# Attention and two expert networks on one core: the second network's weights prepared in alternating units, with five split tiles and merged stores

## The chip, the core and the metric

The kernel runs on one core of a Trainium2 chip. The core has a matrix engine (TensorE, PE in the profile, with its weight loads as PEld), three engines for elementwise work (VectorE or DVE, ScalarE or ACT, GpSimd or POOL), and SyncE (SP), which here only issues DMAs. ACT issues DMAs too, between its own instructions. The metric is the time on the device in microseconds (us), median of several runs.

## The reference

Attention with 8 batches, 8 heads, 576 positions and 64 channels is followed by two networks on 4608 tokens of width 512. All inputs are float32.

```python
def _attn_ref(q, k, v):
    q_s = softmax(q, axis=-1)            # over the 64 channels
    k_s = softmax(k, axis=2)             # over the 576 positions
    kv = np.einsum('bhsd,bhse->bhde', k_s, v)
    return np.einsum('bhsd,bhde->bhse', q_s, kv)

def _moe_ref(x, w_in, w_out):            # 512 -> 2048 -> 512
    r = np.maximum(x @ w_in, 0.0)
    return (r * r) @ w_out

def _moe2_ref(x, w_gate, w_val, w_out, rms_g):   # 512 -> 1536 -> 512
    xn = x / np.sqrt(np.mean(x * x, axis=-1, keepdims=True) + 1e-06) * rms_g
    g, val = xn @ w_gate, xn @ w_val
    return (g / (1 + np.exp(-g)) * val) @ w_out
```

(The two softmax calls stand for the written-out maximum, exponential and division of the reference.)

## The kernel before

Every product is done in float32r with both operands split into a high and a low half (`a = hi + lo`), in three passes: hi x hi, hi x lo, lo x hi (`PASSES`). A split is a copy by ACT, which rounds to the high half, and a subtraction by DVE, which gives the low half.

The tokens are cut into 9 blocks of 512. For blocks 0 to 6 the first network runs in units `(j, c)`, 16 to a block, numbered `i = 16 * j + c`: `p1_A` is the product with a column of `w_in` (12 matmuls into `ps_h`), `p1_hi` and `p1_lo` take relu (`r`), square (`r`) and the split (`w`) on ACT and DVE one unit later, and `p1_B` multiplies by `w_out` into `acc` two units later. The attention of a later block runs in small steps between these (`attention(2 * i)` and `attention(2 * i + 1)` in each unit): `ke` and `qt` are exponentials on ACT, `mcb`, `qm`, `qs`, `qn`, `kt` come from DVE, and PE does `ps_kb`, `ps_q`, `ps_kv` and `ps_x`. The last two blocks and the whole second network use a scheme with 7 products for 8, with sums of halves of the weights in place of the weights.

Weights come in as 64-bit numbers in their words and have to be made into float32 and split first. `d_load` fetches a raw tile of 512 KB (SP), `d_words` makes two words' tiles of it (ACT), `d_float` a float32 tile (DVE, three passes). `tick` does one such step for several tiles, each at its own stage. For the first network this is done in blocks 0 and 1, and the split tiles are kept in DRAM as `wd_i` and `wd_o`. For the second network 36 steps follow in blocks 1 to 5; `n_ticks(i)` says by which unit how many have been done. After four of them `d_quad` has four quarters `a11` to `a22` of a weight and puts eleven entries into the queue `outs`: four sums on DVE (`s1` to `s4`) and seven splits (`d_out`). `d_light` does the like for the first network's weights, whose sums are needed for the last two blocks: it takes a tile that `p1_A` or `p1_B` has just used, adds its halves on DVE, and puts four subtractions and two splits into `sums_l`.

A split by `d_out` writes a tile `so` of 512 KB, one of four that are taken in turn: ACT copies, DVE subtracts at the unit's end (`lows`), and `send` puts it in the list `late`, from which `flush` issues the store on ACT's queue in the next unit: to `wl_i` or `wl_o` (the first network's sums), to `wd_v` (the second network's output weights), or to `wd_t` (its input weights: 42 tiles, the halves of each go to two places in two DMAs of 256 KB). SP loads all of them back later through a ring of 7 tiles `ws`.

Within an engine the instructions run in the order in which the code emits them. A unit emits, in this order: `p1_A`, `p1_hi` of the unit before, `attention(2 * i)`, `p1_B`, `p1_lo`, the steps of the preparation, `flush`, up to three entries of `sums_l` and up to two of `outs` (three in block 6), `attention(2 * i + 1)`, and `lows`. Each DMA, of SP or ACT, counts its landing on one of eight counters, in turn, and waits at its issue until the one before it on that counter has landed.

Of the kernel before, what the change touches and what calls it, by code (L numbers as in the profile page):

```python
# [8 lines left out]
F32 = mybir.dt.float32  # L9
F32R = mybir.dt.float32r  # L10
# [4 lines left out]
ALU = mybir.AluOpType  # L15
# [25 lines left out]
def attention_moe_kernel(  # L41
# [14 lines left out]
    ve, se, ge, te = (  # L56
        InOrder(tc, engine, pinned) for engine in (nc.vector, nc.scalar, nc.gpsimd, nc.tensor)
    )
    B, H, S, D = q.shape
    NT, DM = out.shape  # L60
    P = 128
# [5 lines left out]
    FF1 = w_in.shape[0]  # L67
    NQ = 2 * w_gv.shape[2] // 3
# [5 lines left out]
    const = ctx.enter_context(tc.tile_pool(name="const", bufs=1))  # L74
# [7 lines left out]

    ident = const.tile([P, P], F32, name="ident")
    ones_r = const.tile([P, P], F32R, name="ones_r")
    neg_r = const.tile([P, P], F32R, name="neg_r")
    eps_sb = const.tile([P, 1], F32, name="eps_sb")
    g_sb = const.tile([P, KD], F32, name="g_sb")
    mask = const.tile([P, 2, D], F32, name="mask")
# [12 lines left out]
    turns = {"a": 0, "so": 0, "d": 0, "t": 0}  # L101
# [40 lines left out]
    PROD = ("a11", "s2", "s1", "a12", "s3", "s4", "a22")  # L142
# [16 lines left out]
    def spread(keys, n):  # L159
# [5 lines left out]
    wd = {  # L165
        key: tc.dram_tile([P, 1024], F32, name="wd_" + "_".join(map(str, key)))
        for key in order1 + order2
    }
    SUMS = {"i": ("s2", "s4", "s3", "s1"), "o": ("s2", "s3", "s4", "s1")}
    wsum = {n: tc.dram_tile([P, 4, FF1 // 2, 512], F32, name=f"wl_{n}") for n in SUMS}  # L170
    pools = {}
# [23 lines left out]
    def flat(t):  # L195
        return t.rearrange("p b f -> p (b f)").bitcast(F32)
# [98 lines left out]
    def d_float(key):  # L295
        s, n = words.pop(key)
        if key[0] in ("i", "o"):
            turns["t"] += 1
            t = pools["d"].tile([P, 512], U32, tag=f"t{turns['t'] % 2}", name="t", bufs=1)
        else:  # L300
            n2 = 2 if key[0] in ("12", "21") else 1
            t = pools["q"].tile([P, 512], U32, tag=f"t{key[0]}", name=f"t{key[0]}", bufs=n2)
        sb = s.bitcast(U32)
        ve.tensor_scalar(
            out=t,
            in0=sb,
            scalar1=3,
            scalar2=0x7FFFFFFF,
            op0=ALU.logical_shift_left,
            op1=ALU.bitwise_and,  # L310
        )
        ve.scalar_tensor_tensor(
            out=t, in0=sb, scalar=0x80000000, in1=t, op0=ALU.bitwise_and, op1=ALU.bitwise_or
        )
        ti = t.bitcast(I32)
        ve.tensor_tensor(out=ti, in0=ti, in1=n, op=ALU.add)
        floats[key] = t.bitcast(F32)
# [6 lines left out]
    def flush(all=False):  # L324
        for x in late:
            x[0] -= 1
        while late and (late[0][0] < 0 or all):
            _, key, t = late.pop(0)
            if key[0] in ("i", "o"):
                tc.keep_in_program_order(se.dma_start(out=wd[key], in_=flat(t)))  # L330
                continue
            if key[0] == "L":
                _, kind, x, n = key
                tc.keep_in_program_order(
                    se.dma_start(
                        out=wsum[kind][:, 2 * x : 2 * x + 2, n],
                        in_=flat(t).rearrange("p (g f) -> p g f", g=2),
                    )
                )
                continue  # L340
            if key[1] >= NQ:
                to = [wd["v", BPROD.index(key[0]) * NQ // 2 + key[1] - NQ]]
            else:
                to = []
                for g in range(2):
                    p, at = divmod(g * NS + PROD.index(key[0]), 2)
                    to.append(wd["t", key[1], p][:, at * 512 : (at + 1) * 512])
            for g, o in enumerate(to):
                src = flat(t) if len(to) == 1 else flat(t)[:, g * 512 : (g + 1) * 512]
                tc.keep_in_program_order(se.dma_start(out=o, in_=src))  # L350

    def d_hi(key):
        t = slot_tile(key) if key in res1 else ring_tile()
# [15 lines left out]
    def d_light(kind, j, c):  # L369
        n, r = divmod(c, 2)  # L370
        if (kind, j) not in (("i", 2 + n % 2), ("o", 4 + n % 2)):
            return
        t = pools["d"].tile([P, 512], U32, tag=f"t{r}", name="t", bufs=1).bitcast(F32)
        w = wt[kind, c].bitcast(F32)
        ve.tensor_tensor(out=t, in0=w[:, 0], in1=w[:, 1], op=ALU.add)
        halves_l[r] = t
        if r == 0:
            return
        f = [halves_l.pop(0), halves_l.pop(1)]
        half = [f[0][:, 0:HF], f[0][:, HF:], f[1][:, 0:HF], f[1][:, HF:]]  # L380
        a11, a12, a21, a22 = half if kind == "i" else (half[0], half[2], half[1], half[3])

        def sub(out, in0, in1, op=ALU.subtract):
            sums_l.append(lambda: ve.tensor_tensor(out=out, in0=in0, in1=in1, op=op))

        sub(a22, a21, a22, ALU.add)
        sub(a21, a11, a21)
        sub(a11, a22, a11)
        sub(a12, a12, a11)
        for x in (1, 0):  # L390
            d_out(("L", kind, x, n), lambda x=x: f[x], sums_l)

    def d_out(key, f, outs=outs):
        def run():
            turns["so"] += 1
            t = pools["q"].tile([P, 2, 512], F32R, tag=f"so{turns['so'] % 4}", name="so", bufs=1)
            src = f().rearrange("p (g f) -> p g f", g=2)
            ts = t.rearrange("p g (a f) -> p g a f", a=2)
            se.activation(out=ts[:, :, 0], in_=src, func=AF.Copy)

            def low():
                ve.tensor_tensor(
                    out=ts[:, :, 1], in0=src, in1=ts[:, :, 0].bitcast(F32), op=ALU.subtract
                )
                send(key, t, 0)

            lows.append(low)

        outs.append(run)

    def d_quad(key):
        n, c = key
        if n != "11":
            return
        f = {"a" + b: floats.pop((b, c)) for b in ("11", "12", "21", "22")}

        def d_sum(name, in0, in1, op):
            def run():
                f[name] = pools["q"].tile([P, 512], F32, tag=name, name=name, bufs=1)
                ve.tensor_tensor(out=f[name], in0=f[in0], in1=f[in1], op=op)  # L420

            outs.append(run)

        def out(name):
            d_out((name, c), lambda: f[name])

        d_sum("s1", "a21", "a22", ALU.add)
        out("a22")
        d_sum("s3", "a11", "a21", ALU.subtract)
        d_sum("s2", "s1", "a11", ALU.subtract)  # L430
        out("a11")
        out("s1")
        out("s3")
        d_sum("s4", "a12", "s2", ALU.subtract)
        out("s2")
        out("a12")
        out("s4")
# [332 lines left out]
        return pool.tile([P, 512], F32, tag=tag, name=name)  # L770

    qfs, kT, eks = ({} for _ in range(3))
    qps = []

    def s_loadvl(j):
        nc.sync.dma_start(
# [58 lines left out]
    def s_xn(j, hp):  # L835
        t, ps = xts[j, hp]
        if j == 0:
            f = s_tile([P, T], "xf", 2)
            se.activation(out=f, in_=ps, func=AF.Copy)
            xts[j, hp] = t, f  # L840
        else:
            te.matmul(ps, neg_r, t[:, 0], start=False, stop=True, skip_group_check=True)

    def s_xl(j, hp):
        t, f = xts[j, hp]
# [101 lines left out]
    def p1_hi(j, c):  # L947
        if not ahead(j, ("i", c)):
            p1_r(j, c)
        r = kept.pop((j, c))  # L950
        ghl[1, j, c] = r
        split_hi(ghl, (1, j, c), g_tile(c % 4))
# [418 lines left out]
    def n_ticks(i):  # L1371
        if i < FF1:
            return min(NJ1 + 3, 4 + sum(d <= i for d in due.values()))
        at = [2 * FF1 - 1]
        at += [n for n in range(2 * FF1, 5 * FF1) if n % 4 > 1 or n in (48, 49, 64, 65)]
        at += [n for n in range(5 * FF1, JU * FF1) if n % 4 > 1 or n in (80, 81)]
        at = at[: 4 * NC2 + 1]
        return NJ1 + 4 + sum(n <= i for n in at)

# [59 lines left out]
    with ExitStack() as ctx_a:  # L1439
# [23 lines left out]
        for j in range(2):  # L1463
            t = s_tile([P, 2 * NP, D], f"vl{j}", 1)
            ge.memset(t[SR:P], 0.0)
            vl.append(t)
        make_identity(nc, ident)
        ge.tensor_scalar(
            out=neg_r, in0=ident, scalar1=-1.0, scalar2=0.0, op0=ALU.mult, op1=ALU.add
        )  # L1470
# [110 lines left out]
        for i, (j, c) in enumerate(units[: JU * FF1]):  # L1581
# [24 lines left out]
            p1_A(j, c)  # L1606
            for x in last:
                p1_hi(*x)
            if c == LAG:
                p1_out(j - 1)  # L1610
            attention(2 * i)
# [8 lines left out]
            if j == 1 and 4 <= c < 4 + NTAG:  # L1620
                key = res1[c - 4]
                tc.keep_in_program_order(nc.sync.dma_start(out=wd[key], in_=flat(wt[key])))
            while ticks[0] < n_ticks(i):
                tick()
            if ticks[0] > NJ1 + 4:
                flush()
            for queue, n in ((sums_l, 3), (outs, 2 if j < JU - 1 else 3)):
                for _ in range(min(n, len(queue))):
                    queue.pop(0)()
            attention(2 * i + 1)  # L1630
# [159 lines left out]
```

## Time and profile before

| | us |
|---|---|
| median of 3 runs | 1702.78 (1701.0 to 1706.39) |
| profiled execution | 1712.44 |
| its span, first to last instruction | 1710.7 |
| PE busy in the span | 1656.7 (97%) |
| VectorE busy | 1222.2 (71%) |
| ScalarE busy | 876.8 (51%) |
| moved by DMA | 434.09 MB, mean 254 GB/s |

Shares of busy time are means over the whole program, which has parts of different kinds: the start with the first attention heads, the units of blocks 0 to 6 up to about 757 us, and the second scheme from there to the end. A stretch has to be read for itself. The line of a helper (L34) stands for nearly every instruction, so that groups are told apart by what they write and read, `out<-in`. "Idle before, released by" says what ended the last wait; ACTq and SPq are the queues' own instructions, DMA issues among them. PEclk is the granted clock of TensorE.

### The profile page before, as it was taken

Reading aid. Unit: us, or ns where it says so; the run is one execution under the profiler, and the core shown is the slowest. Engines: PE = TensorE matmul, PEld = TensorE weight load, DVE = VectorE, ACT = ScalarE, POOL = GpSimd, SP = SyncE. Lnnn points to the kernel's source line nnn. Section 1 sums busy time; section 2 is a strip of 40 time slices with the busy share of each in tenths; the row PEclk is TensorE's granted clock in tenths of the full one; section 3 lists DMA queues with packets and bytes.
Section 4 is the critical chain, followed back from the end, with each engine's and each line's share of the span. In section 5 each row is a group of like instructions: output and inputs, shape, how many; then the busy total and the mean of one; then the engine's idle time right before and its main releaser. Section 6 shows DMA issues by size and latency. Waiting matters only on the chain.

```text
span 1710.7 us, 23162 instructions
## 1 busy us (share of the span) xinstructions
PE 1656.7 (97%) x8190; PEld 1367.9 (80%) x8190; DVE 1222.2 (71%) x1936; ACT 876.8 (51%) x1414; POOL 25.0 (1%) x41
## 2 busy tenths in 40 slices
PE   7999999988889999999999999999999999999999
PEld 4888887776667787888788888888888888888898
DVE  7986467877877887445786678667866786668666
ACT  7875445646555565348745444444444444423433
POOL 5000000000000000000000000000000000000000
PEclk9999999999999999999999999999999999999999
DMA  8987989999999998546668556865686558555798
GB/s 259 314 288 251 296 258 306 331 357 313 304 322 315 329 351 272 202 149 214 187 198 278 192 185 202 271 203 186 190 267 216 188 188 256 202 190 195 230 393 302
DMA packets 224898, 434.09 MB, mean 254 GB/s; under 512 B 86416, under 2 KB 117136, under 8 KB 223632
## 3 DMA queue, kind: packets, MB, share of 16 engines
q1 hardware_dynamic: 197088, 369.82, 66.5%
q10 hardware_dynamic: 27696, 62.79, 9.7%
q8 instruction: 66, 1.08, 0.2%
q14 instruction: 48, 0.39, 0.1%
HBM read 347.08 MB, written 85.46 MB: 253 GB/s over the span
## 4 chain that ended last, share of the span: by engine, by line
PE 77%; DMA 11%; DVE 6%; ACT 4%; issue 1%; SPq 0%; ACTq 0%; POOL 0%; POOLq 0%; DVEq 0%
PE ps_x L34 21%; PE ps_y L34 18%; PE ps_h L34 11%; PE acc L34 10%; PE ps_v L34 10%; PE ps_w L34 5%; DMA wd_t<-so 3%; DMA qt<-in_q 2%; DVE t L34 1%; DMA wl_o<-so 1%; DVE so L34 1%; ACT r L34 1%; DMA ws<-wd_i 1%; DMA raw<-in_w_gv 1%; DMA wd_v<-so 1%
## 5 line engine op out<-in xcount | busy, mean ns | idle before, releaser
L34 PE MATMUL ps_h<-x,ws 128*128 128x512 f32 x1008 | 249.5, 398 | 8.6 <-ACT r L34 8.6
L34 PE MATMUL acc<-w,ws 128*128 128x512 f32 x1008 | 248.3, 396 | 0.0
L34 PEld LDWEIGHTS ps_h<-x,ws 128*128 128x128 f32 x1008 | 190.1, 191 | 50.1 <-ACT r L34 10.2
L34 PEld LDWEIGHTS acc<-w,ws 128*128 128x128 f32 x1008 | 189.3, 190 | 39.7
L34 PE MATMUL ps_y<-xo,ws 128*128 128x512 f32 (+1 forms) x816 | 194.3, 373 | 0.3 <-ACT sa L34 0.3
L34 PE MATMUL ps_v<-xo,ws 128*128 128x512 f32 (+1 forms) x816 | 194.1, 373 | 0.2
L34 PE MATMUL ps_x<-ob,ws 128*128 128x512 f32 x768 | 177.4, 389 | 0.0
L34 PE MATMUL ps_x<-xo,ws 128*128 128x512 f32 (+1 forms) x720 | 169.0, 370 | 0.0
L34 PEld LDWEIGHTS ps_y<-xo,ws 128*128 128x128 f32 x816 | 145.0, 188 | 29.1 <-ACT sa L34 0.8
L34 PEld LDWEIGHTS ps_v<-xo,ws 128*128 128x128 f32 x816 | 144.9, 188 | 29.2 <-issue 0.3
L34 PEld LDWEIGHTS ps_x<-ob,ws 128*128 128x128 f32 x768 | 144.2, 188 | 30.0
L34 DVE TENSOR_TENSOR u<-ps_y,p 128x512 f32<-128x512 f32 (+1 forms) x136 | 87.5, 643 | 104.9 <-PE ps_y L34 77.8
L34 ACT ACTIVATE ob<-gs 128x1024 fp32r<-128x1024 f32 (+1 forms) x105 | 102.2, 974 | 113.1 <-PE ps_x L34 52.1
L34 PEld LDWEIGHTS ps_x<-xo,ws 128*128 128x128 f32 x720 | 127.1, 188 | 24.5
L34 DVE TENSOR_TENSOR ob<-gs,ob 128x1024 fp32r<-128x1024 f32 (+1 forms) x105 | 116.7, 1112 | 30.0 <-ACT ob L34 29.5
L34 PE MATMUL ps_y<-ob,ws 128*128 128x512 f32 x576 | 133.8, 390 | 0.7 <-DVE ob L34 0.7
L34 ACT ACTIVATE p<-ps_x 128x512 f32<-128x512 f32 (+1 forms) x74 | 41.7, 564 | 174.6 <-PE ps_x L34 172.3
L34 PEld LDWEIGHTS ps_y<-ob,ws 128*128 128x128 f32 x576 | 107.9, 188 | 24.2 <-DVE ob L34 1.9
L34 DVE TENSOR_TENSOR w<-r,w 128x512 fp32r<-128x512 f32 x112 | 76.9, 687 | 52.9 <-ACT w L34 52.6
L34 ACT ACTIVATE r<-ps_h 128x512 f32<-128x512 f32 x112 | 66.0, 589 | 60.9 <-PE ps_h L34 56.8
L34 PE MATMUL ps_w<-xo,ws 128*128 128x512 f32 (+1 forms) x408 | 97.1, 373 | 0.0
L34 ACT ACTIVATE silu<-silu 128x512 f32<-128x512 f32 (+1 forms) x90 | 49.4, 583 | 75.0 <-DVE silu L34 75.0
(178 smaller groups left out, 2386.2 us busy)
## 6 DMA issues: line engine op xcount, KB each, us to landing
ws<-wd_t SPq DMA_DIRECT2D x210, 512.0 KB, 3.5
ws<-wd_v SPq DMA_DIRECT2D x105, 512.0 KB, 3.3
ws<-wd_o SPq DMA_DIRECT2D x72, 512.0 KB, 5.9
ws<-wd_i SPq DMA_DIRECT2D x64, 512.0 KB, 5.4
wd_t<-so ACTq DMA_DIRECT2D x84, 256.0 KB, 5.9
raw<-in_w_gv SPq DMA_DIRECT2D x36, 512.0 KB, 6.2
wd_v<-so ACTq DMA_DIRECT2D x21, 512.0 KB, 6.7
x<-x2d SPq DMA_DIRECT2D x9, 1024.0 KB, 7.0
```

The costliest lines, as they stand in the source:

```text
L34: ins = f(*args, **kw)
```

## The change

- `n_ticks`: the steps of the second network's preparation stand in the units with `n % 4 > 1` in block 2, `n % 4 < 2` in blocks 3 and 4, and `n % 4 > 1` again from block 5 on. The extra steps in units 48, 49, 64 and 65 are gone. There are still 36 and one, and the last stands in unit 99 (91 before).
- The main loop: two entries of `sums_l` a unit (three before), and of `outs` one in a unit that had a step and three in one that had none (two before, three in block 6). `flush` stands right behind `p1_hi`, ahead of `attention(2 * i)` and `p1_B`.
- `d_out`: five tiles `so` under one tag in place of four. The buffer of `t21` is one in place of two, and `neg_r` lies in a pool that is closed after the start.
- `w_t[n]`: the seven `wd_t` tiles of a weight column group are slices of one DRAM tile, so that both halves of a split tile go out in one DMA of 512 KB.
- `d_light` emits a split as soon as its half is complete; in `d_quad` `s3` comes before the split of `a22`.

```diff
+    w_t = [tc.dram_tile([P, 2 * NS, 512], F32, name=f"w_t{n}") for n in range(NQ)]
+    for n in range(NQ):
+        for p in range(NS):
+            wd["t", n, p] = w_t[n][:, 2 * p : 2 * p + 2].rearrange("p g f -> p (g f)")
...
-            n2 = 2 if key[0] in ("12", "21") else 1
+            n2 = 2 if key[0] == "12" else 1
...
-            if key[1] >= NQ:
-                to = [wd["v", BPROD.index(key[0]) * NQ // 2 + key[1] - NQ]]
+            if key[1] < NQ:
+                to = w_t[key[1]][:, PROD.index(key[0]) :: NS]
+                src = flat(t).rearrange("p (g f) -> p g f", g=2)
             else:
-                to = []
-                for g in range(2):
-                    p, at = divmod(g * NS + PROD.index(key[0]), 2)
-                    to.append(wd["t", key[1], p][:, at * 512 : (at + 1) * 512])
-            for g, o in enumerate(to):
-                src = flat(t) if len(to) == 1 else flat(t)[:, g * 512 : (g + 1) * 512]
-                tc.keep_in_program_order(se.dma_start(out=o, in_=src))
+                to, src = wd["v", BPROD.index(key[0]) * NQ // 2 + key[1] - NQ], flat(t)
+            tc.keep_in_program_order(se.dma_start(out=to, in_=src))
...
-        sub(a12, a12, a11)
-        for x in (1, 0):
-            d_out(("L", kind, x, n), lambda x=x: f[x], sums_l)
+        if kind == "i":
+            d_out(("L", kind, 1, n), lambda: f[1], sums_l)
+            sub(a12, a12, a11)
+            d_out(("L", kind, 0, n), lambda: f[0], sums_l)
+        else:
+            d_out(("L", kind, 0, n), lambda: f[0], sums_l)
+            sub(a12, a12, a11)
+            d_out(("L", kind, 1, n), lambda: f[1], sums_l)
...
-            turns["so"] += 1
-            t = pools["q"].tile([P, 2, 512], F32R, tag=f"so{turns['so'] % 4}", name="so", bufs=1)
+            t = pools["q"].tile([P, 2, 512], F32R, tag="so", name="so", bufs=5)
...
         d_sum("s1", "a21", "a22", ALU.add)
+        d_sum("s3", "a11", "a21", ALU.subtract)
         out("a22")
-        d_sum("s3", "a11", "a21", ALU.subtract)
...
-        at += [n for n in range(2 * FF1, 5 * FF1) if n % 4 > 1 or n in (48, 49, 64, 65)]
-        at += [n for n in range(5 * FF1, JU * FF1) if n % 4 > 1 or n in (80, 81)]
+        at += [n for n in range(2 * FF1, 3 * FF1) if n % 4 > 1]
+        at += [n for n in range(3 * FF1, 5 * FF1) if n % 4 < 2]
+        at += [n for n in range(5 * FF1, JU * FF1) if n % 4 > 1 or n < 5 * FF1 + 2]
...
             for x in last:
                 p1_hi(*x)
+            if ticks[0] > NJ1 + 4:
+                flush()
...
+            before = ticks[0]
             while ticks[0] < n_ticks(i):
                 tick()
-            if ticks[0] > NJ1 + 4:
-                flush()
-            for queue, n in ((sums_l, 3), (outs, 2 if j < JU - 1 else 3)):
+            for queue, n in ((sums_l, 2), (outs, 1 if ticks[0] > before else 3)):
```

What this makes of ACT's order can be seen at two places. In unit 58, in block 3, ACT has these rows before (`w` is the split of the unit, `ke` and `qt` are exponentials of the attention, `s` and `n` the words of a raw tile, `so` a split for a store; DMAHW0 to 7 are the eight landing counters):

```order
L34 ACTIVATE w<-r 128x512 [waits Activation_49]
L34 ACTIVATE ke<-kt 128x640 [waits DVE_49]
L34 ACTIVATE s<-raw 128x512
L34 ACTIVATE n<-raw 128x512
L34 DMA wd_t_1_143<-so 128x512 [waits DMAHW1_49,DVE_49]
L34 DMA wd_t_5_147<-so 128x512 [waits DMAHW4_49]
L34 DMA wd_t_2_144<-so 128x512 [waits DMAHW6_49,DVE_49]
L34 DMA wd_t_6_148<-so 128x512 [waits DMAHW7_49]
L34 ACTIVATE qt<-qt 128x512 [waits DVE_49]
```

And these from the `wl_i` store of unit 58 on in the changed kernel:

```order
L34 DMA wl_i<-so 128x2x512 [waits DMAHW0_49,DVE_49]
L34 ACTIVATE ke<-kt 128x640 [waits DMAHW2_49]
L34 ACTIVATE so<-s_3888 128x2x256
L34 ACTIVATE so<-t_3425 128x2x256 [waits DMAHW3_49]
L34 ACTIVATE so<-s_4012 128x2x256
L34 ACTIVATE qt<-qt 128x512 [waits DMAHW5_49,DVE_49]
L34 ACTIVATE r<-ps_h 128x512 [waits PE_49]
L34 ACTIVATE r<-r 128x512 [waits Activation_49]
L34 ACTIVATE w<-r 128x512 [waits Activation_49]
L34 DMA w_t_150<-so 256x1x512 [waits DMAHW0_49,DVE_49]
L34 DMA w_t_150<-so 256x1x512 [waits DMAHW2_49,DVE_49]
L34 DMA w_t_150<-so 256x1x512 [waits DMAHW6_49,DVE_49]
```

The four issues of `wd_t` behind `n` and ahead of the exponential have become three of `w_t` in unit 59, right behind its `w`; the step with `s` and `n` has gone from these units, and three splits stand in its place.

In unit 103, in block 6, ACT has these rows before:

```order
L34 ACTIVATE w<-r 128x512 [waits Activation_49]
L34 ACTIVATE x<-ps_x 128x512 [waits PE_49]
L34 ACTIVATE r<-ps_h 128x512 [waits DVE_49]
L34 ACTIVATE r<-r 128x512 [waits Activation_49]
L34 ACTIVATE w<-r 128x512 [waits Activation_49]
```

And these in the changed kernel:

```order
L34 ACTIVATE w<-r 128x512 [waits Activation_49]
L34 DMA wd_v_135<-so 128x1024 [waits DVE_49]
L34 DMA wd_v_132<-so 128x1024 [waits DMAHW4_49,DVE_49]
L34 ACTIVATE so<-s_6961 128x2x256 [waits DMAHW5_49]
L34 ACTIVATE x<-ps_x 128x512 [waits PE_49]
L34 DMA wd_v_144<-so 128x1024 [waits DMAHW6_49,DVE_49]
L34 ACTIVATE r<-ps_h 128x512
L34 ACTIVATE r<-r 128x512 [waits Activation_49]
L34 ACTIVATE w<-r 128x512 [waits Activation_49]
```

The last tiles of the preparation, `wd_v`, are split and stored here, where none was before; the third one goes out at the start of unit 104.

## Rows read from the trace of the kernel before

**Rows 1.** The page: busy time, and the span in 40 slices.
```profile
PE 1656.7 (97%) x8190; PEld 1367.9 (80%) x8190; DVE 1222.2 (71%) x1936; ACT 876.8 (51%) x1414; POOL 25.0 (1%) x41
...
PE   7999999988889999999999999999999999999999
```

**Rows 2.** Busy time by stretch, one per block, 2 to 6; columns in the first row.
```profile
core 0: us, PE busy (x) PEld busy (x) DVE busy (x) ACT busy (x) POOL busy (x), PEclk, DMA share, GB/s
220.40:318.20 97.80, 95.95 (x509) 79.27 (x508) 70.28 (x135) 55.32 (x97) 0.00 (x0) 1.00 0.89 299
318.20:431.30 113.10, 100.53 (x511) 81.23 (x510) 87.28 (x164) 66.93 (x117) 0.00 (x0) 0.97 0.97 333
431.30:551.40 120.10, 105.08 (x554) 84.70 (x553) 93.03 (x179) 66.64 (x117) 0.00 (x0) 0.94 0.93 314
551.40:655.00 103.60, 99.61 (x521) 81.97 (x519) 84.36 (x161) 60.45 (x106) 0.00 (x0) 0.98 0.99 331
655.00:757.00 102.00, 99.40 (x482) 81.77 (x482) 54.75 (x93) 48.17 (x82) 0.00 (x0) 0.98 0.59 199
```

**Rows 3.** PE's waits in blocks 3 and 4: us in total, times, longest.
```profile
PE ps_h L34 <- ACT r L34: 8.6, 4, 2.9
PE ps_kb L34 <- DVE x L34: 7.5, 2, 5.2
...
PE ps_q L34 <- DVE qn L34: 2.6, 1, 2.6
```

**Rows 4.** ACT in blocks 3 and 4: two groups (idle before), then waits.
```profile
L34 ACT ACTIVATE so<-t 128x512 fp32r<-128x512 f32 x30 | 18.2, 625 | 46.2 <-DMA raw<-in_w_gv 11.8 <-DVE t L34 5.7 <-issue 5.7
...
L34 ACT ACTIVATE so<-s 128x512 fp32r<-128x512 f32 x20 | 12.5, 628 | 28.4 <-DMA wd_t<-so 11.8 <-DMA qt<-in_q 6.6 <-DMA wl_o<-so 3.4
...
ACT so L34 <- DMA wd_t<-so: 15.6, 7, 3.8
ACT so L34 <- DMA raw<-in_w_gv: 11.8, 3, 5.9
...
ACT so L34 <- DMA qt<-in_q: 6.6, 1, 6.6
...
ACT so L34 <- DMA wl_i<-so: 5.0, 3, 3.6
...
ACT so L34 <- DMA ws<-wd_i: 4.7, 2, 4.0
```

**Rows 5.** Timeline around unit 58: start, length, engine, what, [idle before <- released by].
```profile
390.49 0.69 DVE L34 TENSOR_TENSOR so<-s,so 128x512 fp32r<-128x512 f32 x1 [0.33 <-ACT so L34]
...
392.15 0.63 ACT L34 ACTIVATE w<-r 128x512 fp32r<-128x512 f32 x1
...
394.07 7.59 ACTq L34 DMA_DIRECT2D wd_t<-so  x4
...
401.70 0.63 ACT L34 ACTIVATE qt<-qt 128x512 f32<-128x512 f32 x1 [7.14 <-DMA wd_t<-so]
...
402.87 3.02 PE L34 MATMUL ps_h<-x,ws 128*128 128x512 f32 x12 [2.48 <-ACT r L34]
```

**Rows 6.** DMA of block 3, then block 5: ACT's queue (packets, MB, share), issues.
```profile
q10 hardware_dynamic: 7213, 13.34, 32.0%
...
wd_t<-so ACTq DMA_DIRECT2D x36, 256.0 KB, 6.1
...
q10 hardware_dynamic: 4171, 12.25, 30.5%
...
wd_v<-so ACTq DMA_DIRECT2D x18, 512.0 KB, 6.8
```

**Rows 7.** Issues of `wd_t` in blocks 3 and 4: ns, min/median/max.
```profile
L34 ACTq DMA_DIRECT2D wd_t<-so x70: 326/343/2691, 320.9 to 538.2; - x70
```

**Rows 8.** Who waited for `so` in blocks 3 and 4: us, times.
```profile
  DVE so L34: 31.9, 18
```

More of the change, by code (lines that the diff above doesn't have):

```diff
@@ L84, in attention_moe_kernel @@
     ones_r = const.tile([P, P], F32R, name="ones_r")
-    neg_r = const.tile([P, P], F32R, name="neg_r")
     eps_sb = const.tile([P, 1], F32, name="eps_sb")
@@ L167, in attention_moe_kernel @@
         for key in order1 + order2
+        if key[0] != "t"
     }
+    w_t = [tc.dram_tile([P, 2 * NS, 512], F32, name=f"w_t{n}") for n in range(NQ)]
+    for n in range(NQ):
+        for p in range(NS):
+            wd["t", n, p] = w_t[n][:, 2 * p : 2 * p + 2].rearrange("p g f -> p (g f)")
     SUMS = {"i": ("s2", "s4", "s3", "s1"), "o": ("s2", "s3", "s4", "s1")}
@@ L772, in attention_moe_kernel @@
     qfs, kT, eks = ({} for _ in range(3))
-    qps = []
+    qps, negs = [], []
     def s_loadvl(j):
@@ L841, in s_xn @@
         else:
-            te.matmul(ps, neg_r, t[:, 0], start=False, stop=True, skip_group_check=True)
+            te.matmul(ps, negs[0], t[:, 0], start=False, stop=True, skip_group_check=True)
     def s_xl(j, hp):
@@ L1467, in attention_moe_kernel @@
         make_identity(nc, ident)
+        neg_r = pools["s"].tile([P, P], F32R, tag="neg_r", name="neg_r", bufs=1)
+        negs.append(neg_r)
         ge.tensor_scalar(
```

## The prediction

> **What bounds the kernel now.** The page's first two sections come first [rows 1]: TensorE (PE) is busy for 97% of the span, and in the 40 slices it is below nine tenths only at the very start and between the ninth and the twelfth slice. The rest of the program has no room. So the second view is the one of the stretches in which the change works: the five blocks 2 to 6 of the first network (16 units each), taken from the first `ps_h` matmul of each block to that of the next [rows 2]. Two losses can be read there for each block: the length less PE's busy time, and the part of the clock that was not granted (PEclk below 1.00, times the length). Block 2: 97.80 - 95.95 = 1.9 us and no clock lost. Block 3: 113.10 - 100.53 = 12.6 us, and 0.03 x 113.1 = 3.4 us of clock. Block 4: 15.0 and 0.06 x 120.1 = 7.2 us. Block 5: 4.0 and 2.1 us. Block 6: 2.6 and 2.0 us. Without these losses every block would take 96 to 98 us (95.9, 97.1, 97.9, 97.5, 97.4). All that can be gained is their sum, 50.8 us, and 38.2 us of it lie in blocks 3 and 4.
>
> Who PE waits for comes next [rows 3]: in blocks 3 and 4 above all for ScalarE's `r` and VectorE's `x` and `qn`, and in no row for a weight load. Both engines have time left (ScalarE, ACT, is busy for 66.93 of block 3's 113.10 us, VectorE, DVE, for 87.28 [rows 2]), so they are not too slow; something holds them. What holds ACT is in the fourth view [rows 4]: it stood idle for 46.2 and 28.4 us ahead of the `so` splits, and what ended the idle time was mostly a DMA: a store of `so` (15.6, 5.0), but as often a transfer that `so` has nothing to do with, `raw` 11.8, `qt` 6.6, `ws` 4.7. The order of the program tells why: every DMA, of SP and of ACT, counts its landing on one of eight counters (DMAHW0 to 7), taken in turn, so that a store on ACT can't be issued before the DMA some eight places earlier has landed. One case in full [rows 5]: in unit 58 four issues of `wd_t` take 7.59 us, the query's exponential behind them starts 7.14 us late, the `r` that frees PE's bank comes after it, and PE stands for 2.48 us.
>
> The last view is the transfers [rows 2, 6]: in blocks 3 to 5 the 16 DMA engines are busy for 0.97, 0.93 and 0.99 of the time. So the DMA engines are nearly full as well, and this limits what a freed ACT can give.
>
> **The change part by part.** *One transfer for two.* Blocks 3 and 4 issue 70 `wd_t` stores of 256 KB for 35 tiles, 36 of them in block 3 [rows 6, 7]; afterwards a tile is one issue of 512 KB. An issue takes 343 ns [rows 7], so 35 fewer are 12 us less of ACT's queue, off the path by itself. What counts is the landing wait: 35 DMAs of the two blocks no longer take a counter. A store of 512 KB lands in 6.8 us (`wd_v`) where one of 256 KB took 6.1 [rows 6], so the merged one holds its counter little longer than one half did. Block 5, whose tiles go to `wd_v` in one transfer each, shows what this is worth: the same 18 tiles as block 3, DMA engines as full, and 6.1 us lost instead of 16.0 and 22.2.
>
> *Alternating units.* The preparation's steps for the second network (load, words, float: two ACT and three DVE passes) stand in blocks 3 and 4 in the units in which also the sums of the first network's weights begin; block 2 and block 5, where they fall in different units, lose 1.9 and 6.1 us. Afterwards they are in different units in all four blocks, with at most one `outs` entry in a unit that has a step and three in one that has none. No instruction is added by that. At most three tiles are stored in a unit and never four `wd_t` issues in a row behind two of `wl`.
>
> *Later end.* Blocks 3 and 4 lose the two extra steps each, and the last step moves from unit 91 to 99. Counted in the order of the changed program, the blocks 2 to 6 store 7, 15, 14, 17 and 10 tiles where they store 7, 18, 17, 18 and 3 now (so in the order; the 36 `wd_t` issues and 18 `wd_v` of [rows 6] are the 18 and 18); of the raw loads, which stand two steps ahead of their words, block 3 loses one, block 4 two, and block 5 gets three. A tile of 512 KB costs the engines 32.0% of 113.1 us for 13.34 MB on ACT's queue in block 3, which is 36.2 us for 25.4 tiles, 1.42 us each; in block 5 30.5% of 103.6 us for 12.25 MB, 1.35 us [rows 6]. I take 1.4.
>
> *Five `so` tiles, stores first in the unit.* A tile is held from its split to the landing of its store. The fifth and the earlier issue take away the waits for own stores (15.6 + 5.0 us of ACT in blocks 3 and 4 [rows 4]); no work is added. The price is that ACT now waits for landing and for DVE's low half in front of the attention steps of the same unit instead of behind them: between nothing, if DVE is done by then, and what the last rival below says. I take nothing, since `r`, its square and `w` of the unit stand between (`w` alone 0.63 us [rows 5]). `t21` with one buffer: its readers `s1` and `s3` both run on DVE ahead of the next write, and `s3` has been moved up, so nothing. `neg_r` only changes its place; nothing. The new layout of `w_t` leaves packets of 2 KB in the stores and 4 KB in the loads; the second network's loads run while PE is at nine tenths or more in every slice [rows 1], so up to some tenths of a us on each they cost nothing.
>
> *The sum.* ACT's holdings go, and then the DMA engines are what is late next. Their work now, share times length: block 3 0.97 x 113.1 = 109.7 us, block 4 111.7, block 5 102.6, block 6 60.2. Afterwards block 3: three tiles and one load less, 109.7 - 5.6 = 104.1; block 4: three and two less, 104.7; block 5: one tile less, three loads more, 105.4; block 6: seven tiles more, 70.0. At the share of block 5, 0.99, which is the highest of the rows and was reached with 4.0 us of PE idle, they take 105.2, 105.8 and 106.5 us, and block 6 stays (0.59 goes to some 0.69). Gain: 7.9 + 14.3 - 2.9 = 19.3 us. At a share of 1.00 it would be 22.6 us. If blocks 3 and 4 lost just the 6.1 us that block 5 loses now (9.9 and 16.1 us less than today) and block 5 took 2.9 us more, it would be 23.1 us. At 0.95, the mean of blocks 3 and 4 now, 6 us.
>
> The Trainium skill (DMA: Bandwidth & Descriptors, section Specifications) gives about 358 GB/s as what one core gets of HBM. No block here comes above 333 [rows 2], so the trace doesn't speak against it, nor show that it is reached. By that figure what is left of block 3's 333 GB/s x 113.1 us = 37.7 MB, less 4 x 0.52, or 35.6 MB, would take 99 us instead of my 105.2; that is the third case below.
>
> The profiled execution took 1712.4 us (span 1710.7 and 1.7 around it); 19.3 off gives 1693. The median, 1702.8, is 9.7 lower. If those 9.7 us are losses of the same kind, they are gone from 50.8 already, and the gain shrinks by a fifth to 16; if they are the profiler's, the median drops by the whole. By the sums 19.3, 22.6 and 23.1, and less a little for this, I take 20 off the median: 1683 us.
>
> **The rivals.** (1) *The DMA engines keep the share they have.* For it: the eight counters stay, transfers land no sooner, and block 5 gets work on top of a 0.99. Against it: block 5 reached its 0.99 with the same eight. At 0.95 the gain is 6 us: 1697, with some spread 1692 to 1699.
> (2) *Nothing that decides is touched.* ACT's waits in blocks 3 and 4 were ended as much by loads as by stores (11.8 + 6.6 + 4.7 us against 15.6 + 5.0) [rows 4]. If the loads, which SP issues late because it waits for their buffers, set the pace, the merged store waits for the same load at the same time, and the time stays within 1699 to 1707. Against it: block 2 and block 5 have the same loads and lose little.
> (3) *More than forecast.* A packet's price falls when less is queued, and blocks 3 to 5 move their some 35 MB in 98 to 100 us, 360 GB/s where the fullest now moves 333 [rows 2]. Each then loses only what block 2 does: 99.4, 99.8 and 99.4 us, a gain of 13.7 + 20.3 + 4.2 = 38 us: 1665 (1660 to 1675). The figure of the Trainium skill named above would give about this. Against it: block 5 took 103.6 us for 331 GB/s x 103.6 us = 34.3 MB.
> (4) *Slower: the stores at the head of the unit wait for DVE.* The low half of a split (0.69 us [rows 5]) is the last thing that DVE gets in a unit, behind the attention's DVE steps, and the store now stands behind `w` in the next one. DVE's low halves waited for ACT for 31.9 us in 18 cases in blocks 3 and 4 [rows 8], so the two engines run close behind each other. With three splits a unit the low halves take 3 x 0.69 = 2.1 us. Some 12 storing units in each of three blocks, each 2.1 us late: 75 us of ACT, ahead of exponentials and copies that PE waits for. In blocks 3 and 4 ACT's 75 us in front of `so` went with 38 us lost by PE, half of it. That is 37 us against 20 of gain: 1720. It decides from some 1.1 us a storing unit. Against it: in the unit above, the last low half ended at 391.2 us and `w` at 392.8 us [rows 5], so DVE was 1.6 us early.
>
> **How the numbers follow.** Forecast (1676 to 1691) 0.56; the share stays 0.16, of which 0.10 are faster by over 0.3% (5.1 us, about what a measurement of this kernel tells from no change) and 0.06 are not; nothing touched 0.07; more than forecast 0.14; slower 0.07. Faster 0.56 + 0.14 + 0.10 = 0.80, within 0.3% 0.06 + 0.07 = 0.13, slower 0.07. The range 1669 to 1698 leaves out half of the third rival (0.07), the fourth (0.07) and most of the second (0.06).
>
> **What would show it.** Right: blocks 3 and 4 at 103 to 107 us with a DMA share of 0.97 or more, PEclk at 0.98 or more, ACT's idle time ahead of `so` in them below half of 74.6 us and seldom ended by `w_t`; block 5 a few us longer than now; block 6 as now. Wrong by rival 1 or 2: shares and idle times stay. Wrong by rival 4: idle time of ACT ahead of the attention's exponentials and copies, ended by DVE `so`. If blocks 3 and 4 shrink to 100 us or less at a share below 0.95, the DMA term was too dear and rival 3 holds. A loss in the units from 104 on, where the tiles that were the splits' are given out anew, would be a cost that I put at nothing.

## The result, and the profile after

The changed kernel takes 1680.0 us (median of 4 runs, 1673.86 to 1680.84) where the kernel before takes 1704.59 (4 runs): a ratio of 0.985, with a 95% interval of 0.982 to 0.987. Forecast were 1683 us, faster, within 1669 to 1698. The profiled execution took 1680.51 us, its span is 1678.7 us.

The page's two lines that answer [rows 1], from the profile of the changed kernel: engine busy time, and PE in 40 slices of the span.

```profile
PE 1646.9 (98%) x8190; PEld 1361.9 (81%) x8190; DVE 1219.2 (73%) x1936; ACT 876.5 (52%) x1414; POOL 25.0 (1%) x41
...
PE   6999999999999999999999999999999999999999
```

The dent between the ninth and the twelfth slice is gone. By block, as in [rows 2] (stretch, length, busy time of the engines with the number of instructions, granted clock, DMA share, GB/s), the changed kernel reads:

```profile
core 0: us, PE busy (x) PEld busy (x) DVE busy (x) ACT busy (x) POOL busy (x), PEclk, DMA share, GB/s
221.00:316.70 95.70, 95.70 (x509) 79.33 (x508) 70.82 (x137) 55.53 (x97) 0.00 (x0) 1.00 0.91 307
316.70:417.30 100.60, 97.62 (x510) 80.44 (x510) 79.13 (x149) 63.22 (x111) 0.00 (x0) 0.98 0.98 348
417.30:521.70 104.40, 99.85 (x555) 80.56 (x553) 88.83 (x174) 63.26 (x111) 0.00 (x0) 1.00 0.99 343
521.70:625.00 103.30, 99.81 (x521) 82.08 (x519) 82.46 (x157) 59.72 (x105) 0.00 (x0) 0.98 1.00 336
625.00:725.40 100.40, 97.99 (x482) 80.68 (x482) 65.83 (x114) 55.30 (x94) 0.00 (x0) 1.00 0.71 241
```

Blocks 2 to 6 last 95.7, 100.6, 104.4, 103.3 and 100.4 us instead of 97.8, 113.1, 120.1, 103.6 and 102.0. That is 32 us of span between these two executions, 28.2 of them in blocks 3 and 4. Outside the five blocks nothing has changed: block 2 begins at 221.0 us (220.4 before), and what is left of the spans is 1174.3 us (1174.1 before). The medians differ by less, by 24.6 us, because the profiled execution of before lay 7.8 us above its median.

A block's length in a single execution is not exact. In the profiles of four kernels below that hardly differ from the changed one (`a_four`, `a_late`, `a_tiny`, `a_tinyact`) block 3 lasts 96.4 to 102.7 us, block 4 103.4 to 107.0 and block 5 102.0 to 104.2.

PE's waits in blocks 3 and 4 (us in total, times, longest), against [rows 3]:

```profile
PE ps_kv L34 <- ACT ke L34: 3.0, 1, 3.0
PE ps_kb L34 <- DVE x L34: 2.1, 2, 1.9
PE ps_x L34 <- DVE qT L34: 1.0, 1, 1.0
PE ps_h L34 <- ACT r L34: 0.9, 1, 0.9
```

The wait for `r`, 8.6 us before, is 0.9. ACT's idle time ahead of the `so` splits there, against the two groups of [rows 4] (busy us, mean ns, idle us before and what ended it), and the merged store's issue (ns, min/median/max), against [rows 7]:

```profile
L34 ACT ACTIVATE so<-t 128x512 fp32r<-128x512 f32 x28 | 17.4, 626 | 17.4 <-DVE t L34 10.2 <-DMA wl_o<-so 3.1 <-DVE s L34 2.4
L34 ACT ACTIVATE so<-s 128x512 fp32r<-128x512 f32 x18 | 10.8, 620 | 4.4 <-DMA x2d<-e 4.4
...
L34 ACTq DMA_DIRECT2D w_t<-so x30: 520/527/1375, 328.9 to 521.3; - x30
```

74.6 us have become 21.8. So far nearly all is as the forecast said (block 3 is shorter than its 103 to 107 us). The experiments show that several of its reasons are not the ones that count, or can't be shown to be.

### The profile page after: what moved, and what is told of

Same layout as the page of the kernel before. It is cut to its first block, busy times and chain, and to the rows that moved or that the text cites. A ratio compares the mean times of both kernels' runs of the same rounds, so it can differ in the third digit from the quotient of the medians.

```text
span 1678.7 us, 23124 instructions
## 1 busy us (share of the span) xinstructions
PE 1646.9 (98%) x8190; PEld 1361.9 (81%) x8190; DVE 1219.2 (73%) x1936; ACT 876.5 (52%) x1414; POOL 25.0 (1%) x41
## 3 DMA queue, kind: packets, MB, share of 16 engines
q8 instruction: 66, 1.08, 0.3%
## 4 chain that ended last, share of the span: by engine, by line
PE 77%; DMA 9%; DVE 8%; ACT 4%; issue 1%; SPq 0%; ACTq 0%; POOL 0%; POOLq 0%; DVEq 0%
PE ps_x L34 22%; PE ps_y L34 18%; PE acc L34 10%; PE ps_h L34 10%; PE ps_v L34 10%; PE ps_w L34 5%; DMA kT<-in_k_t 3%; DVE t L34 2%; DMA qt<-in_q 1%; DMA ws<-wd_i 1%; DMA vt<-in_v 1%; DVE so L34 1%; DVE w L34 1%; ACT so L34 1%; PE ps_kv L34 1%
## 5 line engine op out<-in xcount | busy, mean ns | idle before, releaser
L34 PE MATMUL ps_h<-x,ws 128*128 128x512 f32 x1008 | 245.6, 394 | 0.9 <-ACT r L34 0.9
L34 DVE TENSOR_TENSOR u<-ps_y,p 128x512 f32<-128x512 f32 (+1 forms) x136 | 87.4, 642 | 104.3 <-PE ps_y L34 76.9
L34 PE MATMUL ps_w<-xo,ws 128*128 128x512 f32 (+1 forms) x408 | 97.1, 373 | 0.0
```

Source lines behind the costliest of these rows:

```text
L34: ins = f(*args, **kw)
```

## The experiments

Ratios are against the kernel before, measured on the same chip as each run, with their 95% intervals; the changed kernel's is 0.9846 (0.9819 to 0.9873). One per cent is 17 us, and differences to the changed kernel are taken from the ratios.

**Which part is worth what.** Four kernels: each of the two large parts taken out of the changed kernel, and each alone in the kernel before.

`a_two`, the changed kernel with two stores a tile:

```diff
-                to = w_t[key[1]][:, PROD.index(key[0]) :: NS]
+                for g in range(2):
...
+                        se.dma_start(
+                            out=w_t[key[1]][:, g * NS + PROD.index(key[0])],
+                            in_=flat(t)[:, g * 512 : (g + 1) * 512],
+                        )
```

> The changed kernel, with each w_t tile stored again by two DMAs of 256 KB. Counter theory (ACT is held because each issue waits for the landing of the DMA eight places earlier): 35 more DMAs in blocks 3 and 4 bring back a third to half of their lost holdings, so 6 to 10 us over the changed kernel's 1680, 1686 to 1690, with ACT idle ahead of so and PE gaps back in blocks 3 and 4. Schedule theory (the gain is that steps, sums and bytes left blocks 3 and 4; issues do not matter): 1678 to 1682. Rival that the one transfer is all of it: 1700 to 1705.

Measured: 1688.19 us, 0.9905 (0.9884 to 0.9925), so 10 us over the changed kernel.

`b_one`, the kernel before with the merged store alone (the `w_t` lines of the change's diff):

> The kernel before with one change: each w_t tile goes out in one DMA of 512 KB. Counter theory: 8 to 12 us below 1704.6, so 1692 to 1697, fewer and shorter holdings of ACT ahead of so in blocks 3 and 4. Schedule theory: 1702 to 1706. If it is all of it: 1680.

Measured: 1696.07 us, 0.9948 (0.9930 to 0.9966), so 9 us under the kernel before. The merged store is worth 9 to 10 us with or without the rest.

`a_sched`, the changed kernel with `n_ticks`, the queues' counts and the order of the sums in `d_light` of before; and `b_sched`, the kernel before with those of the changed one:

> The changed kernel with the steps in the units of before (the last in unit 91), three entries of sums_l and two or three of outs a unit, and the order of the sums of before; one transfer, five tiles and early stores stay. DMA-work theory: blocks 3 and 4 again carry the work of 3 more tiles and 1 to 2 more raw loads each, 5.6 and 7 us of the DMA engines, and steps and sums meet in one unit; 8 to 14 us over the changed kernel, 1688 to 1694. Counter theory alone: 2 to 4 us, 1682 to 1684. If the schedule is all of it: 1700 to 1705.

> The kernel before with one change: steps, sums and splits in the units of the changed kernel (the last step in unit 99, two entries of sums_l, one or three of outs, the sums' order); four tiles, two DMAs a tile, late stores. DMA-work theory: 10 to 14 us below 1704.6, 1690 to 1695, blocks 3 and 4 shorter, block 5 somewhat longer. Counter theory alone: 2 to 4 us, 1700 to 1703. If it is all of it: 1680.

Measured: `a_sched` 1691.75 us, 0.9924 (0.9907 to 0.9941), 13 us over the changed kernel; `b_sched` 1685.93 us, 0.9892 (0.9873 to 0.9912), 18 us under the kernel before, more than expected. The schedule is the larger part, and the two add up to the whole (0.52% and 1.08% alone, 1.54% together), so that nothing that could be measured is left over for the other parts.

**What of the schedule.** The prediction had put weight on two things in it: steps and sums in different units, and work that leaves blocks 3 and 4. Two kernels from the one before do one each, with its counts for the queues.

```diff
 b_end99:
-        at += [n for n in range(2 * FF1, 5 * FF1) if n % 4 > 1 or n in (48, 49, 64, 65)]
+        at += [n for n in range(2 * FF1, 5 * FF1) if n % 4 > 1]
 b_phase:
-        at += [n for n in range(2 * FF1, 5 * FF1) if n % 4 > 1 or n in (48, 49, 64, 65)]
+        at += [n for n in range(2 * FF1, 3 * FF1) if n % 4 > 1]
+        at += [n for n in range(3 * FF1, 5 * FF1) if n % 4 < 2 or n in (50, 51, 66, 67)]
```

> The kernel before without the extra steps in units 48, 49, 64 and 65, so that the last step stands in unit 99 as in the changed kernel; steps and sums of blocks 3 and 4 still share their units, and the queues' counts are those of before. The whole schedule alone gave 18.6 us (b_sched). If it is the work moved out of blocks 3 and 4: 11 to 16 us, 1689 to 1695. If it is the alternating: 0 to 5 us, 1700 to 1706.

> The kernel before with the steps of blocks 3 and 4 in the other units (n % 4 < 2), the four extra ones too (50, 51, 66, 67): alternating with the sums, the last step in unit 91 as before, the queues' counts as before. If the schedule's gain is the work moved out of blocks 3 and 4: 0 to 5 us, 1700 to 1706. If it is the alternating: 11 to 16 us, 1689 to 1695.

Measured: `b_end99` 1694.15 us, 0.9936 (0.9916 to 0.9955); `b_phase` 1705.1 us, 1.0001 (0.9989 to 1.0013). Blocks 3, 4 and 5 of `b_end99`, then 3 and 4 of `b_phase`:

```profile
317.20:418.40 101.20, 98.07 (x511) 80.28 (x510) 76.81 (x145) 61.76 (x110) 0.00 (x0) 0.98 1.00 341
418.40:531.20 112.80, 102.20 (x555) 83.12 (x553) 90.33 (x175) 63.68 (x112) 0.00 (x0) 0.97 0.92 314
531.20:637.80 106.60, 100.57 (x522) 81.92 (x519) 87.93 (x168) 63.46 (x112) 0.00 (x0) 0.98 1.01 345
...
317.90:435.80 117.90, 103.60 (x511) 83.24 (x510) 90.07 (x169) 67.41 (x119) 0.00 (x0) 0.94 0.96 331
435.80:548.00 112.20, 100.99 (x554) 82.09 (x553) 93.79 (x181) 66.95 (x118) 0.00 (x0) 0.97 0.98 336
```

Four steps fewer in blocks 3 and 4 are worth 11 us: these blocks get shorter (113.1 and 120.1 before; up to 7.8 of the 19 us between the profiles is that of before), and block 5 pays up to 3 us for it. Putting the steps into the other units, with the same four extra ones, is worth nothing as a whole: in its profile block 3 is longer and block 4 shorter. That does not rule the alternating out. By the edit's lists the steps of `b_phase` stand in eight units running, 46 to 53, where the kernel before has six (46 to 51) and the changed one four (46 to 49), and its four extra ones fall into the sums' units; a gain could be hidden behind that. What the whole schedule gives beyond the later end, 0.44%, or some 7 us, lies in the counts of the queues, the order of the sums and the alternating together. Which of them it is was not separated.

**The small parts.** `a_four` has `bufs=4` for `so`; `a_late` has `flush` behind the steps again.

> The changed kernel with four so tiles in place of five. With three splits in a unit and their stores at the head of the next, the first of them is landed (some 7 us after its issue) before the fourth and fifth are wanted, mostly: 1 to 4 us over the changed kernel, 1680 to 1684. If the fifth tile is what keeps ACT going: 1688 or more.

> The changed kernel with the stores issued behind the unit's steps, as before, not behind p1_hi. A tile is held half a unit (3 us) longer, but ACT's attention steps of the unit's first half no longer stand behind the stores: between 2 us better and 4 us worse, 1678 to 1684. If the early issue is an own source of gain: 1686 or more; if ACT's waits at the head of the unit cost (the rival that ends slower): 1675 or less.

Measured: 1678.52 us, 0.9845 (0.9817 to 0.9874), and 1680.07 us, 0.9845 (0.9814 to 0.9875). Neither the fifth tile nor the early issue can be told from nothing. `a_late` shows one thing more, in ACT's groups for its blocks 3 and 4:

```profile
L34 ACT ACTIVATE so<-t 128x512 fp32r<-128x512 f32 x29 | 18.2, 630 | 48.5 <-DVE t L34 20.7 <-DMA ws<-wd_i 6.6 <-DVE kt L34 3.4
L34 ACT ACTIVATE so<-s 128x512 fp32r<-128x512 f32 x18 | 10.8, 619 | 3.1 <-DMA x2d<-e 2.8 <-DMA w_t<-so 0.4
```

ACT stands idle for 51.6 us ahead of `so` instead of 21.8, and the time is the same. Idle time ahead of the splits was a sign that something is late, not a cost. 29.8 of the 52.8 us by which it fell go with the place of the stores in the unit, and were not saved but moved: over all of its instructions ACT idles in blocks 3 and 4 for 77.9 us in the changed kernel and for 78.6 in `a_late` (98.7 before). With the change the idle time ahead of `ke` rose from 7.5 to 18.1 us, and ahead of `kvd` from 0.3 to 8.6.

**Places in the turn, and bytes.** `a_more` and `a_tiny` add a DMA on SP to each raw load of the second network, of 512 KB and of 32 KB, `a_tinyact` one of 32 KB on ACT. They store a resident weight tile, or 64 columns of it, to a place that nothing reads (here `a_more`):

```diff
     def d_load(key):
         n, c = key
+        if n not in ("i", "o"):
+            at = 4 * c + ("12", "21", "22", "11").index(n)
+            w = flat(wt[res1[0]])
+            nc.sync.dma_start(out=extra[at, :, 0:1024], in_=w[:, 0:1024])
```

> The changed kernel with one more DMA for each raw load of the second network (36 in blocks 1 to 5, 8 each in 2 to 5): 512 KB of a resident weight tile to a DRAM tile that nothing reads, on SP. DMA-work theory: 8 x 1.4 = 11 us more work in each of blocks 3 to 5, which are at a share of 0.99, and 2 us beyond the room in block 2: 28 to 35 us over the changed kernel, 1708 to 1715. Counter theory: 32 more places in the turn of eight, some 8 us: 1686 to 1690.

> The same with 32 KB (256 bytes a row) a DMA in place of 512 KB: a place in the turn of the counters, and an issue on SP, without the bytes (0.15 us of the DMA engines each). Counter theory: 5 to 8 us over the changed kernel, 1685 to 1688. DMA-work theory: 0 to 3 us, 1680 to 1683.

Measured: `a_more` 1699.07 us, 0.9962 (0.9946 to 0.9977); `a_tiny` 1679.88 us, 0.9848 (0.9821 to 0.9875). Both missed their aim: nothing held these DMAs in their places, and they went out as early as they could. The first line is of `a_more`, the second of `a_tiny`, the third of `a_tinyact`, where the order was kept (ns, min/median/max; first and last start in us):

```profile
L281 SPq DMA_DIRECT2D extra<-w x36: 319/572/1299, 52.0 to 167.2; - x36
...
L281 SPq DMA_DIRECT2D extra<-w x36: 319/438/1349, 53.5 to 83.4; - x36
...
L34 ACTq DMA_DIRECT2D extra<-w x36: 321/327/1371, 141.4 to 620.2; - x36
```

`a_more` therefore says that 36 tiles of 512 KB in blocks 0 and 1 cost 19 us, 0.5 us each (its block 2 begins at 239.6 us, not 221.0). It says nothing on blocks 3 to 5, and `a_tiny` says nothing on the counters there.

> The changed kernel with one more DMA of 32 KB for each raw load of the second network, as in a_tiny, but issued by ACT in the middle of the unit. On SP the 36 cost nothing. If what the halves of a store cost is ACT's waiting for a counter at the issue: 5 to 9 us over the changed kernel, 1685 to 1689. If it is the bytes or the landing of the halves: 0 to 2 us, 1679 to 1682.

Measured: 1682.42 us, 0.9874 (0.9854 to 0.9895), about 0.3% over the changed kernel, less than the two intervals can tell apart. 42 more halves of a store (`a_two`) cost 0.6%. So the 36 small DMAs on ACT, one a step, can have cost anything from nothing to as much as the halves, and the run does not decide. Whether the halves cost by the places they take, by coming up to six in a row behind a unit with three splits, or by their landing, stays open.

**ACT freed of the stores.** `a_pool` issues the stores of the splits on GpSimd, which has nothing to do there:

```diff
-            tc.keep_in_program_order(se.dma_start(out=to, in_=src))
+            tc.keep_in_program_order(nc.gpsimd.dma_start(out=to, in_=src))
 (and the store of the first network's sums likewise)
```

> The changed kernel with the stores of the second network's tiles and of the first network's sums issued on GpSimd, which is idle there: ACT issues none of them and never waits for a landing counter. If ACT's holdings still cost PE time: 3 to 8 us below the changed kernel, 1672 to 1677. If the DMA engines' work sets blocks 3 to 5 by now: 1678 to 1682. If an issue on GpSimd is so slow that the so tiles are not free in time: 1686 or more.

Measured: 1669.13 us (1668.15 to 1672.39), 0.9788 (0.9769 to 0.9807): 0.6%, some 10 us, below the changed kernel, and the fastest of all. Its blocks 3, 4 and 5, and its issues of `w_t` on GpSimd:

```profile
315.80:413.60 97.80, 96.04 (x510) 79.24 (x509) 76.51 (x145) 61.35 (x107) 14.86 (x21) 1.00 0.96 342
413.60:517.10 103.50, 99.14 (x555) 80.75 (x553) 89.11 (x174) 63.39 (x111) 15.72 (x23) 1.00 1.01 354
517.10:614.80 97.70, 97.70 (x521) 80.98 (x519) 83.64 (x160) 61.65 (x109) 15.28 (x24) 1.00 1.02 359
...
L350 POOL DMA_DIRECT2D w_t<-so x29: 684/690/931, 328.1 to 512.6; - x29
```

In block 5 PE is busy for all of the 97.7 us with the DMA share at 1.02, and the clock is full in all three. So what the changed kernel still loses in block 5 is not the DMA engines' work. Only block 5 lies outside the lengths that the profiles of the changed kernel and its near likes gave above, where ACT issues the stores (102.0 to 104.2 us for block 5); blocks 3 and 4, at 97.8 and 103.5 us, lie within. ACT's waits that a DMA ended fall from 23.0 to 1.6 us in blocks 3 and 4 and from 14.8 to 1.4 in block 5, and PE's two waits of block 5 in the changed kernel, 3.4 us for DVE's `x` and `qT`, are gone. The edit takes two things away at once: ACT's waiting at its issues, and the places that the stores took among the eight counters, since in the program GpSimd's DMAs count on eight others (DMASW0 to 7). Which of the two gives the 10 us was not separated. A third thing changes with it and is small: the stores go out in larger packets (3326 for 12.11 MB in block 5, where ACT's queue had 4848 for 12.06), but a tile's price there goes only from 1.33 to 1.31 us. The gain is above the 3 to 8 us that were expected for ACT's holdings, and the expectation that the DMA engines set these blocks (1678 to 1682) has fallen.

## Why the prediction was right, and where not

**Place and size of the loss: right.** The 50.8 us in blocks 2 to 6 were the whole room, and 38.2 us in blocks 3 and 4 the part that went: 28.2 us of it are back, the clock is granted to 0.98 and 1.00 there, and block 6, which took seven tiles more, did not get longer (100.4 us).

**The sum: its time was right, its bound by the DMA share was not.** The prediction let the DMA engines' work set the blocks at a share of 0.99 and came to 105.2, 105.8 and 106.5 us for blocks 3 to 5. Measured: 100.6, 104.4 and 103.3; in the five profiles with nearly this program block 3 stays below 103 and block 5 below 104.3 us, while 105.8 is within what block 4 shows. The price of a tile held: ACT's queue in block 3 is

```profile
q10 hardware_dynamic: 6028, 11.60, 30.5%
```

which is 30.5% of 100.6 us for 22.1 tiles of 0.524 MB, 1.39 us each, against 1.4 taken. What was wrong is that all the work together is a fixed amount: block 3 was to need 104.1 us of the engines and needed 0.98 x 100.6 = 98.6. A part is bytes, 35.0 MB where 35.6 were reckoned, since two raw loads left the block (10 before, 8 now) and not one; the rest is that a MB took 2.82 us of the engines where it took 2.91 before. And a share of 0.99 is not where PE begins to wait, as `a_pool` shows with 1.02 and no idle PE, and block 3 of `a_tiny`, where ACT issues the stores as in the changed kernel:

```profile
316.80:413.20 96.40, 96.06 (x511) 79.25 (x510) 78.68 (x149) 63.16 (x111) 0.00 (x0) 1.00 1.00 361
```

A full share went with short blocks as well as with long ones; it told what could be expected to become late next, but not at which length. The gain of the profiled executions, 32 us, was put at 19.3.

**The step to the median.** 9.7 us between the profiled execution and the median were weighed as either losses or the profiler's, and the gain was kept at 20. The medians went down by 24.6. In the changed kernel the profiled execution is at the median (1680.5 against 1680.0), which fits losses that vary from run to run; it was not tested. So it is partly luck that 1683 lies within 3 us of the result: the gain of the profiled executions was put 13 us too low, and the 7.8 us by which the one of before stood above its median, which would have made the gain smaller still (16 by the prediction's own working), were hardly taken off.

**One transfer for two: right that it counts, open in how.** The comparison with block 5, where a tile is one transfer, pointed to it, though to far more: block 5 lost 9.9 and 16.1 us less than blocks 3 and 4, and 9 to 10 us came out (`b_one`, `a_two`). The working behind it is borne out in part. The merged store lands 6.7 us after its issue (median in blocks 3 and 4) where a half took 5.7, so that it holds its counter little longer, as was taken. The saving of ACT's issue time is small: a merged issue takes 527 ns where a half took 343, so 30 issues are 15.8 us in blocks 3 and 4 where 60 would have been 20.6: 4.8 us saved, not the 12 us that were worked out for 35 tiles. And the freed places in the turn of the counters could not be shown to be the cause (`a_tinyact`). In `a_two` ACT did wait longer behind the store's issues, which is what one would expect of it (its profile is of its slowest run, 1694.05 us); the longest waits for `w_t` there are (us, times):

```profile
  ACT qT L34: 11.9, 2
  ACT ke L34: 7.8, 1
  ACT kvd L34: 6.3, 1
```

In the changed kernel no step waits for `w_t` by name, but some wait for loads instead, `kvd` for `qt` 5.0 us and `qT` for `ws` 4.9 us. With counters in turn the name of a wait says only whose landing came last.

**Alternating units: not shown to be worth anything.** Blocks 2 and 5 lost little, and in them steps and sums fall in different units; the prediction read one as the reason of the other. `b_phase` gives 1.0001, with its steps crowded at the start of block 3. The two blocks differ from 3 and 4 also in the number of steps (8 where 3 and 4 have 10) and in the number of store issues, and these two did gain when they alone were changed (`b_end99` 11 us, `b_one` 9). Whether the alternating gives a part of the 7 us beyond the later end stays open.

**Later end: right,** and with its sign in each block as far as single profiles tell: shorter in 3 and 4, a little longer in 5 (`b_end99`, 106.6 against 103.6 us), no loss in 6 (99.7 against 102.0). In the changed kernel block 5 is not longer (103.3). With the stores in two again it is 105.4 (`a_two`; 105.3 in `b_sched`), so the merged store seems to make up for it there.

**Five tiles, stores first: wrong that they take anything away.** The 20.6 us of waiting for own stores were ACT's, not the path's (`a_four`, `a_late`). That they cost nothing was right, and the last rival did not occur: the splits' low halves do not hold ACT at the head of the unit for long enough to cost PE anything that can be measured (`a_late` 0.9845).

**The rivals.** Nothing touched and slower did not occur. The rival of more than forecast, a price that falls when less is queued, came true in part in block 3 (98.6 us of work for the 104.1); that less was queued is not shown to be the reason. (What block 2 loses, 1.9 us, on top of block 3's 97.1 is 99.0 us, where that rival's sum has 99.4.) Its rate, 358 GB/s by the Trainium skill (DMA: Bandwidth & Descriptors, section Specifications), is near what the blocks of the faster kernels move: 342, 354 and 359 GB/s in `a_pool`. The runs do not show it as a ceiling: block 3 of `a_tiny` moved 361 GB/s in 96.4 us, `a_more` 406 in the 30 us from 130 us on, and in block 5 of `a_pool` PE never waited, so that the transfers did not set its length.

**What is left.** Moving the stores to GpSimd gives another 10 us, which the prediction's own reading (issues wait for landings) suggests; the DMA bound, put in front of it, had ruled it out.

## What to carry to other kernels

An engine that issues DMAs between its own instructions can stand at an issue for the landing of some other transfer, as ACT did here; an idle engine's queue was the better place for stores, by 10 us, even though an issue takes longer there (690 ns against 527). Idle time ahead of the instruction that waits is no measure of a loss: it moved from 74.6 to 21.8 and to 51.6 us with 25 us of gain and then none. When two stretches differ in several ways, a comparison of them names a suspect only. The single edit that changes one of them is cheap, but has to leave the rest as it was: `b_phase` changed the phase of the steps and crowded them as well. And one profile gives a block's length only to some 3 us either way, so that several have to agree before a block is explained.

## What was not expected of the hardware

An issue of the merged store on ACT takes 527 ns, one of the same 512 KB to `wl_i` on the same queue 366 ns (median of 9 in the changed kernel), and one of 256 KB 343 ns: the time goes with the shape of the access (256 rows in the program, where the `wl_i` store has 128 x 2) and not with the bytes. On GpSimd the same store takes 690 ns, and the stores go out there in larger packets: 3168 for 11.54 MB in block 3, against 6028 for 11.60 MB on ACT's queue. And a DMA share of 1.02 by packets' time, at 359 GB/s, went with a PE that never waited in that block.
